# Moving the tiles that TensorE reads to multiples of 64 bytes, and spacing out the steps of the first block sums

## The chip, the cores and the metric

The kernel runs on one core of a Trainium2 chip. The metric is the device time of one execution in microseconds (us); the runs of one kernel are given by their median and their range. A profile of one execution shows each engine's instructions: PE is TensorE (PEld its weight loads), DVE is VectorE, ACT is ScalarE, POOL is GpSimd, SP issues the DMAs.

## The reference

Three stages follow each other, all in float32.

```python
# q, k, v: (8, 8, 576, 64); p: (8, 8, 32, 64)
p_packed = sm_attn(p, k, v)            # softmax attention of 32 packs per head
out = sm_attn(q, p_packed, p_packed)   # and back to 576 positions
x = out.transpose(0, 2, 1, 3).reshape(4608, 512)

xn = x / sqrt(mean(x * x) + 1e-6) * rms_g
g = xn @ w_gate                        # 512 -> 1536
x = (g * sigmoid(g) * (xn @ w_val)) @ w_out

h = x @ w_in                           # 512 -> 2048
return (h * sigmoid(1.702 * h)) @ w_out2
```

## The kernel before

**Precision.** A float32 value is kept as a rounded high part and a low part (tiles ending in h and l, or a tile with an index for the part), and a product is three matmuls: high by high, high by low, low by high.

**Stages.** The first MLP runs in four units of two batches each, `u` = 0 to 3. In each unit 12 column blocks of 128 follow: `prods` makes the gate and value weights of the unit on PE (ps_w, L668), `gateval` multiplies them with the attention weights (ps_g, L701; tanh on ACT at L708, two steps on DVE at L709 and L711 give the tile th, which is split into Hh on ACT and Hl on POOL), and `project`, called for two blocks at once, multiplies by w_out (ps_o, L732). The attention of the next unit runs between these steps, and so does the conversion of the weights: first those of the first MLP (`piece`), then those of the second (`weights` in `mlp2`), which go through a ring of three buffers with the tag raw (`RAWS`). The last unit has no attention of a next unit beside it; in its place stand the first block sums of the second MLP.

**The second MLP** works on 1024 tokens at a time (four times, then 512 tokens once) and on pairs of blocks of the hidden size (eight). The up product of a pair is a block matrix product in seven instead of eight block products (`up`, ps_up, L999): for this the tokens' inputs are seven tiles x_b11, x_b21, x_b22, x_t1, x_t2, x_t3 and x_t4, four of which are sums or differences of blocks. Each block product is six matmuls with 512 moving columns (256 for the last 512 tokens). The moving operand is the x_ tile, the stationary one a block of the weights (wi, or a staging tile for the first pair). Then `down` (ps_dn, L1062) multiplies the result by w_out2: 48 matmuls of 512 columns per pair (24 for the last 512 tokens), whose moving operand is the tile wo2 and whose stationary one is gh or gl. The down products of a pair are written between the up products of the next.

**The first 1024 tokens' sums** are made in `first_x` during the last unit of the first MLP. It is a generator of 11 steps: loads, splits into high and low part (`split_x`: a cast on ACT, a difference on DVE or POOL), and differences. The main loop calls one step at each step of the first MLP, from the start of the last unit on:

```python
if ahead is not None and u == NU - 1:
    next(ahead, None)
```

One difference goes into `spare()`, a buffer of the raw ring, and is split into x_t4 afterwards; the tile of t2 is free for its own split only once it has been read for that.

**What sets the order.** The kernel is written in one order, but a scheduler, which the framework runs while the program is built, decides where an instruction stands on its engine: one that is ready for its inputs and its buffers can be moved ahead of others that were written before it. Nothing is changed at run time; each engine works through its list.

**PSUM and SBUF.** The first MLP's products have five PSUM banks (pool mm). The pool `at` of attention, and after it the pool `pre` with the seven x_ tiles, lie at the right end of SBUF and are filled from that end; a tile's size therefore sets the address of all the tiles to its left.

Of the kernel before, what the change touches and what calls it, by code (L numbers as in the profile page):

```python
# [9 lines left out]
F32 = mybir.dt.float32  # L10
# [12 lines left out]
def fl(t):  # L23

    return t.bitcast(F32)
# [3 lines left out]
def tile_pack_attention__then__two_mlps(  # L29
# [14 lines left out]
    nc = tc.nc  # L44
    B, H, S, D = q.shape
# [8 lines left out]
    P = 128  # L54
# [16 lines left out]
    FULL = 4  # L71
# [15 lines left out]
    if NT % (2 * TH):  # L87
        spans.append((WHOLE * 2 * TH, NT % (2 * TH) // 2))
    SECOND = 4300.0
    SCALE = 1.0 / math.sqrt(D)  # L90

    dram = ctx.enter_context(tc.tile_pool(name="dram", bufs=1, space=DRAM))
# [46 lines left out]
    def attention(at, first, lp, psum, getL, getAT):  # L139
# [12 lines left out]
        def split(parts, src, engine):  # L152
            nc.scalar.copy(parts[0], src)
            if len(parts) > 1:
                engine.tensor_sub(parts[1], src, fl(parts[0]))
# [225 lines left out]
        def s2(n, e):  # L381
            b, g = chains[n]
            ps = scores(st[n]["ppT"], st[n]["qT"], e)
            if e == 0:
                st[n]["t"] = at.tile([P, S // 32, 32], F32, tag="e", name="t1", bufs=2)
            t = st[n]["t"]
            nc.vector.transpose(t[:, span(e).start // 32 : span(e).stop // 32, :], ps)
            if e == 0:
                return
            bc = [P, S // 32, 32]  # L390
            mx = at.tile([P, S // 32], F32, tag="mx", name="mx")
            nc.vector.tensor_reduce(mx, t, axis=AX.X, op=ALU.max)
            nc.gpsimd.tensor_sub(t, t, mx.unsqueeze(2).to_broadcast(bc))
            nc.scalar.activation(t, t, AF.Exp, scale=SCALE)
            sm = at.tile([P, S // 32], F32, tag="s2", name="s2")
            nc.vector.tensor_reduce(sm, t, axis=AX.X, op=ALU.add)
            nc.gpsimd.tensor_scalar_add(sm, sm, 1e-9)
            r2 = at.tile([P, S // 32], F32, tag="r2", name="r2")
            nc.vector.reciprocal(r2, sm)
            if n != NG:  # L400
                nc.gpsimd.tensor_mul(t, t, r2.unsqueeze(2).to_broadcast(bc))
            st[n]["r2"] = r2

        def weights(n):

            b, g = chains[n]
            A = getAT(b // 2)[b % 2][g]
            if n == NG:

                t = st[n]["t"]  # L410
                with behind(("ri", 0)):
                    nc.gpsimd.tensor_mul(t, t, st[n]["r2"].unsqueeze(2).to_broadcast([P, S // 32, 32]))
            nc.vector.transpose(A, st[n]["t"].rearrange("p t n -> p (t n)"))
            if full(n):
                st[n]["A"] = (A,)
                return
            st[n]["A"] = [at.tile([P, S], F32R, tag=f"A{x}", name=f"A{x}") for x in "hl"]
            split(st[n]["A"], A, nc.gpsimd)

        def x(n, c0):  # L420
# [394 lines left out]
    def mlp2(cv):  # L815
# [77 lines left out]
        def split_x(q, src, engine, n=TH):  # L893
            t = x_tile(q, n)
            nc.scalar.copy(t[:, 0], src)
            engine.tensor_sub(t[:, 1], src, fl(t[:, 0]))

        def first_x():

            t0, n = spans[0]  # L900
            a, b = (
                pools["pre"].tile([P, 2, 2, TH], F32, tag=q, name=f"x_{q}", bufs=1) for q in ("t4", "t2")
            )
            b11, b12, b22, b21 = a[:, 0], a[:, 1], b[:, 0], b[:, 1]
            for t, i0, k in ((b11, 0, 0), (b12, 0, 1), (b22, 2, 1), (b21, 2, 0)):
                load_part(t, i0, t0 + k * n, n)
            yield
            split_x("b11", b11, nc.gpsimd)
            yield
            nc.vector.tensor_sub(b11, b12, b11)  # L910
            nc.gpsimd.tensor_sub(b12, b22, b12)
            yield
            split_x("t1", b11, nc.vector)
            yield
            split_x("t3", b12, nc.gpsimd)
            yield
            split_x("b21", b21, nc.vector)
            yield
            split_x("b22", b22, nc.gpsimd)
            yield  # L920
            nc.vector.tensor_sub(b11, b22, b11)
            yield
            t4 = spare()
            nc.vector.tensor_sub(t4, b21, b11)
            yield
            split_x("t2", b11, nc.gpsimd)
            yield
            split_x("t4", t4, nc.vector)
            yield

        def first_w():
# [176 lines left out]
    pools = {}  # L1108
    with ExitStack():
# [9 lines left out]
        with ExitStack() as st1:  # L1119
# [4 lines left out]
            at = st2.enter_context(tc.tile_pool(name="at", bufs=1, side="right"))  # L1124
# [48 lines left out]
                todo = [calls for _, calls in todo]  # L1173
            starting[0] = False
            pools["main"] = st1.enter_context(tc.tile_pool(name="main", bufs=1, side="left"))
            u, ahead = 0, None
            sources = [mm]
            between = lambda: sources[-1]
            weights, first_x, first_w, second = mlp2(cv)
# [3 lines left out]
            for what in run():  # L1183
# [7 lines left out]
                elif what == "unit":  # L1191
# [4 lines left out]
                    elif u + 1 == NU:  # L1196
                        st2.close()
                        pools["pre"] = ctx.enter_context(tc.tile_pool(name="pre", bufs=1, side="right"))
                        ahead = first_x()
                    spent = 0.0  # L1200
                else:
                    if ahead is not None and u == NU - 1:
                        next(ahead, None)
                    spent += what
                    done += what
                    while todo and spent >= every:
# [5 lines left out]
                    if finished():  # L1212
                        ready += what
                        while ready >= SECOND:
                            ready -= SECOND
                            next(converting, None)
# [50 lines left out]
```

## Time and profile before

| | us |
|---|---|
| median of 3 runs | 1693.5 |
| range of the runs | 1692.46 to 1696.78 |
| profiled execution, time | 1693.33 |
| profiled execution, span of its instructions | 1691.4 |
| attention and first MLP, units 0 to 2 | 0 to about 731 |
| first MLP, last unit | about 731 to 934 |
| second MLP | 934 to 1691.4 |

Times within the profile are microseconds from the start of the span; 1.9 us of the execution lie outside it. A row that gives a line with an L names a line of the kernel; in tile names the buffer numbers are left out, so that x_t stands for x_t1 to x_t4 and x_b for x_b11, x_b21 and x_b22.

### The profile page before, as it was taken

The numbers are of one execution on the slowest core, as the hardware profiler recorded it, in microseconds if no ns is written. First come the engines' busy times: TensorE is split into PE (matmuls) and PEld (weight loads), VectorE is DVE, ScalarE is ACT, GpSimd is POOL, SyncE is SP. The second block draws the span as 40 slices with busy tenths as digits, with TensorE's granted clock in tenths as the row PEclk, the third lists the DMA queues.
The fourth block names the chain that finished last, engine by engine and source line by source line (L and its number), as shares of the span: only waits on it lengthen the run. The fifth ranks groups of instructions, "written<-read, shape, count | busy, mean of one in ns | idle before, by whom it ended". The sixth has DMA issues, their size and how long they took to land.

```text
span 1691.4 us, 25480 instructions
## 1 busy us (share of the span) xinstructions
PE 1649.5 (98%) x9312; PEld 1465.1 (87%) x9312; DVE 1148.6 (68%) x2154; ACT 730.7 (43%) x1586; POOL 719.3 (43%) x680
## 2 busy tenths in 40 slices
PE   7899999999999999989999999999999999999998
PEld 5689998999999999979999788888888888888897
DVE  5788988777878787877765355845584558455755
ACT  4667776666566665555554311321132113211221
POOL 2447777647664566574455211411141114111211
PEclk8999999999999999989999999999999999999999
DMA  9555666575655655466453833443344334333374
GB/s 267 158 174 175 205 185 227 196 231 173 184 206 172 228 170 179 167 212 216 171 194 110 314 137 137 144 162 137 137 153 153 137 137 143 138 137 137 135 267 152
DMA packets 163740, 298.41 MB, mean 176 GB/s; under 512 B 88992, under 2 KB 118688, under 8 KB 148384
## 3 DMA queue, kind: packets, MB, share of 16 engines
q1 hardware_dynamic: 163616, 296.79, 52.1%
q8 instruction: 74, 1.21, 0.3%
q14 instruction: 50, 0.41, 0.1%
HBM read 235.93 MB, written 60.82 MB: 175 GB/s over the span
## 4 chain that ended last, share of the span: by engine, by line
PE 85%; DVE 5%; DMA 3%; ACT 2%; issue 2%; POOL 1%; SPq 1%; DVEq 0%; POOLq 0%; ACTq 0%
PE ps_dn L1062 23%; PE ps_up L999 21%; PE ps_o L732 16%; PE ps_g L701 13%; PE ps_w L668 3%; PE ps_at L299 2%; PE ps_at L344 2%; PE ps_at L288 2%; PE ps_at L432 1%; DMA raw<-in_moe_w_out_dram 1%; SPq L174 1%; DMA vn<-in_v_dram 1%; DVE Wl L673 1%; DVE th L709 1%; DVE th L711 1%
## 5 line engine op out<-in xcount | busy, mean ns | idle before, releaser
L1044 POOL TENSOR_TENSOR gl<-gf,gh 128x512 fp32r<-128x512 f32 (+1 forms) x120 | 148.3, 1237 | 529.8 <-DVE gh L1043 527.9
L1062 PE MATMUL ps_dn<-wo,gh 128*128 128x512 f32 x1152 | 356.4, 393 | 1.1 <-DVE gh L1043 1.1
L732 PE MATMUL ps_o<-Hh,wo 128*128 128x384 f32 x1152 | 323.7, 342 | 11.6 <-DVE th L709 3.5
L1071 DVE TENSOR_TENSOR acc<-acc,ps_dn 128x512 f32<-128x512 f32 x252 | 172.4, 686 | 163.2 <-PE ps_dn L1062 161.9
L1062 PEld LDWEIGHTS ps_dn<-wo,gh 128*128 128x128 f32 x1152 | 214.6, 188 | 49.6 <-DVE gh L1043 1.3
L1041 ACT ACTIVATE gf<-gf 128x512 f32<-128x512 f32 (+1 forms) x120 | 70.8, 590 | 399.9 <-DVE gf L1023 245.6
L701 PE MATMUL ps_g<-Aqh,Wh 128*128 128x288 f32 x768 | 232.8, 304 | 3.3 <-ACT add L745 1.4
L732 PEld LDWEIGHTS ps_o<-Hh,wo 128*128 128x128 f32 x1152 | 212.3, 190 | 16.8 <-DVE th L709 4.1
L701 PE MATMUL ps_g<-Aql,Wh 128*128 128x288 f32 x768 | 226.0, 295 | 0.0
L701 PE MATMUL ps_g<-Aqh,Wl 128*128 128x288 f32 x768 | 225.4, 295 | 0.0
L999 PE MATMUL ps_up<-x_t,wi 128*128 128x512 f32 (+1 forms) x936 | 224.9, 371 | 0.0
L1062 PE MATMUL ps_dn<-wo,gl 128*128 128x512 f32 x576 | 222.0, 390 | 0.0
L732 PE MATMUL ps_o<-Hl,wo 128*128 128x384 f32 x576 | 196.3, 341 | 1.2 <-POOL Hl L718 1.2
L999 PEld LDWEIGHTS ps_up<-x_t,wi 128*128 128x128 f32 x936 | 165.5, 188 | 34.3
L718 POOL TENSOR_TENSOR Hl<-th,Hh 128x576 fp32r<-128x576 f32 x96 | 139.3, 1452 | 118.1 <-ACT Hh L717 115.4
L673 DVE TENSOR_TENSOR Wl<-ps_w,Wh 64x512 fp32r<-64x512 f32 x192 | 131.8, 687 | 68.8 <-ACT Wh L672 65.7
L999 PE MATMUL ps_up<-x_b,wi 128*128 128x512 f32 (+1 forms) x702 | 165.1, 372 | 0.4 <-ACT gf L1041 0.4
L747 POOL TENSOR_TENSOR acc<-acc,add 128x384 f32<-128x384 f32 x135 | 137.3, 1029 | 60.6 <-ACT add L745 59.1
L701 PEld LDWEIGHTS ps_g<-Aqh,Wh 128*128 128x128 f32 x768 | 144.0, 188 | 9.0 <-ACT add L745 1.7
L672 ACT CAST Wh<-ps_w 64x512 fp32r<-64x512 f32 x192 | 111.9, 583 | 85.9 <-PE ps_w L668 59.8
L999 PEld LDWEIGHTS ps_up<-x_b,wi 128*128 128x128 f32 x702 | 123.5, 188 | 26.4 <-issue 0.8
L701 PEld LDWEIGHTS ps_g<-Aql,Wh 128*128 128x128 f32 x768 | 144.3, 188 | 0.0
(185 smaller groups left out, 2995.7 us busy)
## 6 DMA issues: line engine op xcount, KB each, us to landing
wi<-wi SPq DMA_DIRECT2D x35, 1792.0 KB, 7.3
wg<-wg SPq DMA_DIRECT2D x48, 1024.0 KB, 5.7
wo<-wo SPq DMA_DIRECT2D x36, 1024.0 KB, 6.9
wo<-wo SPq DMA_DIRECT2D x48, 512.0 KB, 4.0
raw<-in_moe_w_out_dram SPq DMA_DIRECT2D x28, 512.0 KB, 4.6
wi<-stage SPq DMA_DIRECT2D x24, 512.0 KB, 5.2
x<-acc SPq DMA_DIRECT2D x32, 288.0 KB, 3.0
out_dram<-acc SPq DMA_DIRECT2D x36, 256.0 KB, 2.1
```

Of the source, the lines that this page charges most:

```text
L668: last = nc.tensor.matmul(ps[:, a], st[:, i], mv[:, i], start=n == 0, stop=n == 2)
L672: nc.scalar.copy(Wh[rows, :, g], src)
L673: nc.vector.tensor_sub(Wl[rows, :, g], src, fl(Wh[rows, :, g]))
L701: nc.tensor.matmul(ps, st[:, o, g, c * P : (c + 1) * P], mv[:, g, cols], start=n == 0, stop=n == 3 * NG - 1)
L718: nc.gpsimd.tensor_sub(Hl, th, fl(Hh))
L732: nc.tensor.matmul(ps, st[:, m * P : (m + 1) * P], mv[:, cols], start=n == 0, stop=n == 3 * len(ss) - 1)
L747: nc.gpsimd.tensor_add(a, a, t)
L999: nc.tensor.matmul(bank[b], wt[:, y, k], x[:, z, k], start=c == 0 and not go_on, stop=c == 5, skip_group_check=go_on)
L1041: nc.scalar.activation(gf, src, AF.Gelu_apprx_sigmoid)
L1044: engine.tensor_sub(gl, gf, fl(gh))
L1062: nc.tensor.matmul(ps, st[:, r * P : (r + 1) * P], w[:, i, y], start=c == 0, stop=c == 5)
L1071: nc.vector.tensor_add(acc[m], acc[m], ps)
```

## The change

The diff does two things. In three places it makes a pool 32 bytes a partition larger (the tile s2 grows from 72 to 128 bytes, where it took 96 with its padding; `even` is added to the pool `at` and `even2` to the pool `pre`), which moves the tiles to their left. And a step of `first_x` is called only after each 9000 ns of the loop's own count of matmul time (`CALM`), in place of at each step.

```diff
+    CALM = 9000.0
...
-            sm = at.tile([P, S // 32], F32, tag="s2", name="s2")
+            sm = at.tile([P, P // 4], F32, tag="s2", name="s2")[:, : S // 32]
...
             st[n]["A"] = [at.tile([P, S], F32R, tag=f"A{x}", name=f"A{x}") for x in "hl"]
+            if n == FULL:
+                nc.gpsimd.memset(at.tile([P, 8], F32, name="even"), 0.0)
             split(st[n]["A"], A, nc.gpsimd)
...
             split_x("t4", t4, nc.vector)
+            nc.gpsimd.memset(pools["pre"].tile([P, 8], F32, name="even2"), 0.0)
             yield
...
-            u, ahead = 0, None
+            u, ahead, calm = 0, None, 0.0
...
                     if ahead is not None and u == NU - 1:
-                        next(ahead, None)
+                        calm += what
+                        if calm >= CALM:
+                            calm -= CALM
+                            next(ahead, None)
```

In the built program the seven x_ tiles begin 32 bytes past a multiple of 64 before (x_t4 at 172000, the others 8192 bytes apart from 180192 on) and at a multiple of 64 now (171968, and from 180160 on). The tiles wo2, wi, gh and gl, and all that the first MLP's matmuls read, begin at multiples of 64 in both. In attention the tiles pbm, pTh, pTl, kTl, qTl, vh, vl, aTh, aTl, pp, ppl, ppTl, Ah, Al and the kept ones move from 32 past to a multiple of 64.

The order of the instructions changes less than the loop. This is DVE before, at the start of the last unit; x_t on the left of an arrow at L910 and L921 is a difference of blocks, x_b and x_t at L896 are the low parts of x_b21 and x_t1, Aql and th belong to the first MLP:

```order
L685 TENSOR_TENSOR Aql<-AT_7143,Aqh 128x576
L711 SCALAR_TENSOR_TENSOR th<-th,ps_g 128x288
L910 TENSOR_TENSOR x_t_10094<-x_t_10094 128x1024
L685 TENSOR_TENSOR Aql<-AT_7144,Aqh 128x576
L896 TENSOR_TENSOR x_b_10171<-x_t_10095,x_b_10171 128x1024
L742 TENSOR_TENSOR acc_7469<-acc_7469,ps_o 128x384
L673 TENSOR_TENSOR Wl<-ps_w,Wh 64x2x256
L896 TENSOR_TENSOR x_t_10147<-x_t_10094,x_t_10147 128x1024
L673 TENSOR_TENSOR Wl<-ps_w,Wh 64x2x256
L921 TENSOR_TENSOR x_t_10094<-x_t_10095,x_t_10094 128x1024
```

And this is DVE now at the same place, with the lines three further down:

```order
L688 TENSOR_TENSOR Aql<-AT_7145,Aqh 128x576
L714 SCALAR_TENSOR_TENSOR th<-th,ps_g 128x288
L913 TENSOR_TENSOR x_t_10226<-x_t_10226 128x1024
L688 TENSOR_TENSOR Aql<-AT_7146,Aqh 128x576
L899 TENSOR_TENSOR x_b_10823<-x_t_10227,x_b_10823 128x1024
L745 TENSOR_TENSOR acc_7471<-acc_7471,ps_o 128x384
L676 TENSOR_TENSOR Wl<-ps_w,Wh 64x2x256
L899 TENSOR_TENSOR x_t_10584<-x_t_10226,x_t_10584 128x1024
L676 TENSOR_TENSOR Wl<-ps_w,Wh 64x2x256
L924 TENSOR_TENSOR x_t_10226<-x_t_10227,x_t_10226 128x1024
```

Nothing has moved here: the four instructions of the sums have the same neighbours.

Before, the split of t4 (x_t from spare, at L896) stood on DVE at the end of a step's row of th products, some 30 rows further on, ahead of a weight conversion (between, L119 to L122):

```order
L709 SCALAR_TENSOR_TENSOR th<-th,ps_g 128x288
L711 SCALAR_TENSOR_TENSOR th<-th,ps_g 128x288
L709 SCALAR_TENSOR_TENSOR th<-th,ps_g 128x288
L711 SCALAR_TENSOR_TENSOR th<-th,ps_g 128x288
L896 TENSOR_TENSOR x_t_10233<-spare,x_t_10233 128x1024
L119 TENSOR_SCALAR between<-w 128x512
L120 TENSOR_SCALAR between<-between 128x512
L709 SCALAR_TENSOR_TENSOR th<-th,ps_g 128x288
```

Now the row of th products runs into the conversion without it:

```order
L712 SCALAR_TENSOR_TENSOR th<-th,ps_g 128x288
L714 SCALAR_TENSOR_TENSOR th<-th,ps_g 128x288
L712 SCALAR_TENSOR_TENSOR th<-th,ps_g 128x288
L714 SCALAR_TENSOR_TENSOR th<-th,ps_g 128x288
L120 TENSOR_SCALAR between<-w 128x512
L121 TENSOR_SCALAR between<-between 128x512
L122 SCALAR_TENSOR_TENSOR between<-raw_10173,between 128x512
L712 SCALAR_TENSOR_TENSOR th<-th,ps_g 128x288
```

The difference into spare and the split of t4 now stand on DVE about 100 rows further on, where a step's th products begin after the last low parts of the weights (Wl); acc is an accumulator of the first MLP, sums are sums of weight blocks of the second:

```order
L745 TENSOR_TENSOR acc_10401<-acc_10401,ps_o 128x384 x2
L927 TENSOR_TENSOR spare<-x_t_10227,x_t_10226 128x1024
L676 TENSOR_TENSOR Wl<-ps_w,Wh 64x2x256
L853 TENSOR_TENSOR sums<-sums,w 128x256
L745 TENSOR_TENSOR acc_10401<-acc_10401,ps_o 128x384
L676 TENSOR_TENSOR Wl<-ps_w,Wh 64x2x256
L854 TENSOR_TENSOR sums<-w,sums 128x256
L712 SCALAR_TENSOR_TENSOR th<-th,ps_g 128x288 x2
L676 TENSOR_TENSOR Wl<-ps_w,Wh 64x2x256
L714 SCALAR_TENSOR_TENSOR th<-th,ps_g 128x288 x2
L899 TENSOR_TENSOR x_t_11440<-spare,x_t_11440 128x1024
L712 SCALAR_TENSOR_TENSOR th<-th,ps_g 128x288 x2
```

Between its neighbours here the difference (L927) and the split (L899) are new; the casts that belong to the splits of t2 and t4 on ACT, and the difference of t2 on POOL, have moved to the same place.

## Rows read from the trace of the kernel before

**Rows 1.** The page: PE and the others over the span, granted clock in 40 slices.
```profile
PE 1649.5 (98%) x9312; PEld 1465.1 (87%) x9312; DVE 1148.6 (68%) x2154; ACT 730.7 (43%) x1586; POOL 719.3 (43%) x680
...
PEclk8999999999999999989999999999999999999999
```

**Rows 2.** The page: the chain that ended last, shares by line.
```profile
PE ps_dn L1062 23%; PE ps_up L999 21%; PE ps_o L732 16%; PE ps_g L701 13%; PE ps_w L668 3%; PE ps_at L299 2%; PE ps_at L344 2%; PE ps_at L288 2%; PE ps_at L432 1%; DMA raw<-in_moe_w_out_dram 1%; SPq L174 1%; DMA vn<-in_v_dram 1%; DVE Wl L673 1%; DVE th L709 1%; DVE th L711 1%
```

**Rows 3.** Stretches (from:to, length): busy time by engine, clock, DMA share.
```profile
core 0: us, PE busy (x) PEld busy (x) DVE busy (x) ACT busy (x) POOL busy (x), PEclk, DMA share, GB/s
505.00:545.00 40.00, 39.78 (x278) 38.41 (x277) 33.56 (x70) 25.11 (x60) 18.16 (x19) 1.00 0.50 171
730.00:765.00 35.00, 27.73 (x152) 25.54 (x150) 30.07 (x41) 19.57 (x33) 24.65 (x14) 0.85 0.52 177
765.00:790.00 25.00, 22.94 (x144) 22.51 (x145) 20.15 (x36) 13.38 (x25) 10.61 (x7) 0.93 0.51 179
...
934.00:1600.00 666.00, 665.56 (x2888) 539.87 (x2888) 376.52 (x576) 144.01 (x224) 160.71 (x109) 1.00 0.41 152
...
844.00:857.00 13.00, 13.00 (x92) 13.00 (x91) 11.57 (x21) 8.06 (x18) 7.33 (x8) 1.00 0.68 228
```

**Rows 4.** The chain in order of time, second MLP: start, length, what and count.
```profile
939.86 3.97 PE ps_up L999 x17
...
980.63 1.39 PE ps_dn L1062 x6
982.02 1.40 PE ps_up L999 x6
983.42 2.75 PE ps_dn L1062 x12
...
1004.27 2.75 PE ps_dn L1062 x12
```

**Rows 5.** PE's timeline in a long run of down products: start, length, instruction.
```profile
951.55 0.61 PE L1062 MATMUL ps_dn<-wo,gh 128*128 128x512 f32 x2
...
955.18 0.39 PE L1062 MATMUL ps_dn<-wo,gl 128*128 128x512 f32 x1
955.40 1.80 PE L999 MATMUL ps_up<-x_b,wi 128*128 128x512 f32 x7
```

**Rows 6.** The chain in order of time, first MLP.
```profile
786.36 3.12 PE ps_o L732 x18
789.48 0.71 PE ps_w L668 x6
...
907.89 12.72 PE ps_g L701 x96
920.61 12.49 PE ps_o L732 x72
```

**Rows 7.** The chain in order of time, last 512 tokens of the second MLP.
```profile
1615.17 4.20 PE ps_up L999 x36
...
1625.60 4.20 PE ps_up L999 x36
```

**Rows 8.** Tile x_t, 730 to 800 us: durations ns (min/median/max), first and last start.
```profile
L895 ACT CAST x_t<-x_t x3: 1042/1046/1047, 741.5 to 768.0; 128x1024 fp32r<-128x1024 f32 x3
...
L896 POOL TENSOR_TENSOR x_t<-x_t,x_t x2: 2393/2901/3409, 748.6 to 770.4; 128x1024 fp32r<-128x1024 f32 x2
...
L896 DVE TENSOR_TENSOR x_b<-x_t,x_b x1: 3380/3380/3380, 742.0 to 742.0; 128x1024 fp32r<-128x1024 f32 x1
...
L924 DVE TENSOR_TENSOR spare<-x_t,x_t x1: 1221/1221/1221, 766.7 to 766.7; 128x1024 f32<-128x1024 f32 x1
L895 ACT CAST x_t<-spare x1: 1048/1048/1048, 773.4 to 773.4; 128x1024 fp32r<-128x1024 f32 x1
L896 DVE TENSOR_TENSOR x_t<-spare,x_t x1: 2156/2156/2156, 774.5 to 774.5; 128x1024 fp32r<-128x1024 f32 x1
```

**Rows 9.** PE's waits, 730 to 765 us: us in total, times, longest.
```profile
PE ps_o L732 <- ACT add L745: 2.4, 1, 2.4
```

**Rows 10.** PE's waits, 765 to 790 us.
```profile
PE ps_o L732 <- DVE th L709: 2.0, 1, 2.0
```

## The prediction

> **What bounds the kernel now.** I read the shares of busy time first. PE is busy 98% of the span at a granted clock of nearly ten tenths throughout [rows 1], so the kernel can get faster in two ways only: PE's matmuls follow each other more closely, or the few stretches in which PE stands still go. The chain that ended last says the same: its longest lines, 23% and 21% of the span, are the down and the up products of the second MLP on PE, and the next three are PE's too [rows 2].
>
> The table of stretches shows where PE stands still [rows 3]. In the last unit's opening, 730 to 765 us, PE is busy 27.73 of 35 us at a mean clock of 0.85; from 765 to 790 it is busy 22.94 of 25 us at 0.93. The same passage one unit earlier, 505 to 545 us, is all but full (39.78 of 40, clock 1.00), and so is a stretch later in the last unit, 844 to 857. So what costs there is what only the last unit has, the block sums. In the second MLP, 934 to 1600 us, PE is busy 665.56 of 666 us: there only the pace of the matmuls counts.
>
> **The pace of the matmuls.** The chain in order of time gives it, since a piece divided by its count is the distance from start to start. In a steady iteration of the second MLP [rows 4] six up products take 1.40 us, 233 ns each; a run of 17 at the stage's start takes 3.97 us, also 233 ns, so this is no edge effect. Six down products between them take 1.39 us, 231.7 ns. But a long run of down products is faster: in PE's timeline [rows 5] from the first start at 951.55 us to the next up product at 955.40 there are 17 products in ten rows (the first and the last stand there), 226.5 ns each. That is 6.7 ns less than the up products', for the same 512 moving columns, 128 stationary columns, type and clock, with nothing waited for. What differs: the down products' moving tile (wo2) begins at a multiple of 64 bytes, the up products' (x_...) 32 bytes past one; both stationary tiles begin at a multiple. The down products behind up products share the slower pace for about six matmuls.
>
> Is it only the switch from one product to another? In the first MLP, where all tiles are aligned, ps_o products take 3.12 us for 18 between ps_w products, and 12.49 us for 72 in one run [rows 6]: 173.3 and 173.5 ns. There switching costs nothing.
>
> **The change, part by part. (1) Alignment in the second MLP.** The seven x_... tiles move down by 32 bytes; the counts of products stay. Of 40 iterations 32 have 42 up products of 512 columns, 1344 in all, and 48 down; the last eight have 42 up of 256 columns, 336, and 24 down. One iteration (42 up, 48 down) now takes 20.85 us (983.42 to 1004.27 [rows 4]). If all 90 ran at the pace of the long down run it would take 90 x 0.2265 = 20.39 us, 0.465 us less, and over 32 such iterations 14.9 us. In the eight last iterations, of 256-column up products, one takes 10.43 us (1615.17 to 1625.60 [rows 7]): 36 up in 4.20 us, 116.7 ns, so 42 x 0.1167 + 24 x 0.2265 = 10.34 us, 0.09 us less, together 0.7 us. The bounds are 0 (the gap has another cause) and 15.6 us. I take 15.6: the gap is there from the run at 939.86 us on [rows 4], when the weights still come out of a staging tile and no down product has run yet, and alignment is the one difference that lasts.
>
> A page of the Trainium skill speaks against this: Advanced Engine Details and Errata, section SBUF Cachelines, gives lines of 16 bytes. 32 bytes past a multiple of 64 is still the start of such a line, so by that rule no line more is touched and this term would be zero. The rows show a gap between 226.5 and 233 ns that this rule does not explain, but no run here has yet tied it to the address.
>
> **(2) Alignment in attention.** In the program some 680 matmuls of the attention stages also read a moved tile, all with 320 columns or fewer. The nearest rows are the 256-column products: 116.7 ns with a misaligned x_... tile [rows 7], 118 ns for the aligned ps_w (six in 0.71 us [rows 6]). So I price these at 0. Bounds: 680 x 6.7 ns = 4.6 us gained, or 1.6 ns lost on each and on the 336 short up products, 1.6 us.
>
> **(3) The spread.** The kernel text now asks for a step of the sums every 9 us of matmul work, but the order of the instructions hardly follows. In DVE's order the difference x_t4, the splits into x_b21 and x_t1 and the second difference stand between the same neighbours as before; on ACT and POOL the first five splits do too. These make the stall of 730 to 765 us: one split holds DVE for 3.38 us [rows 8], and of the 7.3 us that PE stands still there [rows 3] most are four waits for DVE and ACT, the longest 2.4 us [rows 9]. I price this at 0 change.
>
> Only what hangs on the ring of three raw buffers moves: the difference into `spare` (1.22 us [rows 8]) and the splits t2 and t4 (on ACT 1.05 us each, on POOL 2.39 at the least, on DVE 2.16 [rows 8]). On DVE they go from 766.7 and 774.5 us to where 850 and 856 us are now.
>
> What goes: at 774.5 us the t4 split holds DVE for 2.16 us just as the last th of a step is due; PE then waits 2.0 us for th [rows 10] and the clock falls. From [rows 3], 25 - 22.94 = 2.1 us idle, and a mean clock of 0.93 over 25 us is 3.5 us at the lower of the two levels, 1.75 us of lost work: 3.8 us.
>
> What comes: from 844 to 857 us DVE is busy 11.57 of 13 us and PE 13.00 [rows 3], and now 1.22 + 2.16 = 3.4 us of DVE work and two 1.05 us casts on ACT are added. Behind them on DVE wait the th products of a gate step and the last Wl, and PE waits for those through the five banks of pool mm. A ps_g group takes 12.72/16 = 0.8 us (96 matmuls [rows 6]), so five banks cover some 3 us of lateness, and the two DVE pieces stand apart with five rows of other work between. Bounds: 0, and 3.4 us plus 1.75 us of lower clock, 5.1 us. I take 1.0 us, near the lower end, because the pieces land at the opening of a step, not at its close. Net gain 2.8 us. Two 32-byte memsets on POOL add nothing: the second waits for a matmul that POOL's next instruction waits behind anyway.
>
> **Sum.** The profiled execution took 1693.3 us, at the median of the runs (1693.5). 1693.3 - 14.9 - 0.7 - 2.8 = 1674.9, so 1675 us.
>
> **Rivals.**
> *The address does not matter.* Then the 6.7 ns belong to the up products for a reason that stays, and only the 2.8 us remain: 1690.5 us. For it: the 256-column products read the same misaligned tiles at no loss. The Trainium skill's rule on lines gives the same. Against it: the pieces in [rows 4, 5]. Chance 0.30.
> *Only the up products heal.* If the down products behind them stay slow because the two alternate, the gain is 1344 x 6.7 ns = 9.0 us: 1693.3 - 9.0 - 2.8 = 1681.5. The runs in the first MLP [rows 6] speak against a price of alternating. Chance 0.10.
> *The moved splits make a new stall.* With the address worth nothing, the upper bound for the new place gives 1693.3 - 3.8 + 5.1 = 1694.6, slower than before. This decides once th is more than some 3 us late at 850 to 860 us, so that PE stands still long enough for the clock to fall. DVE's 1.4 free us of 13 speak for it, the order at the opening of a step against. Chance 0.05.
> *The steps do spread on the chip.* Then the loss of [rows 3] in 730 to 765 us goes as well: 7.3 us idle and 0.15 x 35 us = 5.2 us of clock, and 1675 becomes 1662.5. The order of instructions speaks against it. Chance 0.03.
>
> **How the numbers follow.** The forecast has 0.52, and its own range is 1671 (attention gains too) to 1680. The whole range reaches through the second rival into the first one's lower half: 1671 to 1692. What is left out, under 2 in 10, is the steps spreading, the new stall, and the end of the first rival where the moved splits gain little. No change means within 0.3%, 5.1 us, about what a measurement of this kernel can tell. Forecast, second and last rival lie beyond it: 0.65 faster. The other two lie within, but for 0.02 of worse stalls: 0.33 and 0.02.
>
> **What would show it.** In the chain after, six up products should take 1.36 us, not 1.40, and an iteration 20.4 us, not 20.85. If these pieces stay, the first rival holds. If up falls to 1.36 and down stays at 1.39, it is the second. The windows 730 to 765 us should look as before (the steps still bunched), and 765 to 790 us should reach clock 1.00 without the split on DVE. The moved split should stand near 852 us (what precedes is 3 to 4 us earlier), with PE's waits for th there under 1 us in all. The up products should begin about 3 us before 933.8 us. It would all be wrong if PE's pace were set by something both products share after the change, or if the late splits met a step's close.

## The result and the profile after

The changed kernel takes 1680.8 us (median of 4 runs, 1678.12 to 1680.88) against 1694.6 us of the kernel before (median of 4, 1692.46 to 1696.78): a ratio of 0.9915, 95% interval 0.9897 to 0.9932. The forecast was 1675 us with a range of 1671 to 1692, so the time lies in the range and the sign is right, but it is 5.8 us above the forecast and just outside the forecast's own range of 1671 to 1680. By the time alone the second rival, 1681.5 us, would look right; the trace below rules it out. The profiled execution took 1680.88 us, with a span of 1679.1 us; that is 12.45 us less than the 1693.33 us that the sum of the prediction began with.

Three points in the trace show in which part the time changed: the start of the first up product, the start of the first up product of 256 columns (the last 512 tokens), and the end of the span.

| part | before | after | change | forecast |
|---|---|---|---|---|
| up to the second MLP | 933.79 | 934.85 | +1.06 | -2.8 |
| to the first 256-column up product | 656.77 | 642.81 | -13.96 | -14.9 |
| from there to the end | 100.89 | 101.42 | +0.53 | -0.7 |

So the largest term came as forecast, and both small ones have the wrong sign.

The page after: PE's busy time fell by 12 us and its share stayed (compare [rows 1]).

```profile
PE 1637.6 (98%) x9312; PEld 1467.1 (87%) x9312; DVE 1149.7 (68%) x2154; ACT 729.8 (43%) x1586; POOL 716.0 (43%) x682
```

The chain in order of time in a steady iteration (start, length, what and count), to be read against [rows 4]:

```profile
980.78 1.36 PE ps_dn L1066 x6
982.14 1.36 PE ps_up L1003 x6
983.50 2.72 PE ps_dn L1066 x12
...
1003.90 2.72 PE ps_dn L1066 x12
```

Six up products take 1.36 us, where they took 1.40, and the six down products beside them 1.36, where they took 1.39: both kinds now follow each other at 226.7 ns. An iteration takes 1003.90 - 983.50 = 20.40 us; the forecast was 20.39.

The same view in the last 512 tokens, against [rows 7]:

```profile
1602.26 4.31 PE ps_up L1003 x36
1606.58 2.29 PE ps_dn L1066 x10
...
1612.79 4.31 PE ps_up L1003 x36
```

Here 36 up products take 4.31 us, where they took 4.20: 119.7 ns each in place of 116.7. Down products behind them take 229 ns each, not 226.5. An iteration takes 10.53 us, where it took 10.43.

The stretches of [rows 3] after (busy time by engine, clock, DMA share), and one more, 790 to 930 us:

```profile
core 0: us, PE busy (x) PEld busy (x) DVE busy (x) ACT busy (x) POOL busy (x), PEclk, DMA share, GB/s
505.00:545.00 40.00, 39.78 (x277) 38.40 (x277) 33.39 (x71) 25.18 (x60) 17.86 (x19) 1.00 0.51 176
730.00:765.00 35.00, 27.04 (x147) 24.80 (x145) 30.23 (x41) 18.80 (x33) 23.93 (x13) 0.85 0.53 183
765.00:790.00 25.00, 24.73 (x155) 24.29 (x156) 18.51 (x36) 13.18 (x27) 8.22 (x7) 0.94 0.45 170
844.00:857.00 13.00, 11.45 (x79) 11.21 (x78) 12.40 (x21) 7.92 (x14) 7.55 (x6) 1.00 0.70 246
790.00:930.00 140.00, 136.90 (x927) 135.56 (x927) 93.42 (x174) 71.81 (x143) 73.39 (x64) 1.00 0.47 163
```

The same last stretch in the kernel before:

```profile
790.00:930.00 140.00, 139.43 (x946) 138.44 (x945) 91.44 (x174) 72.00 (x145) 72.27 (x64) 1.00 0.48 167
```

The opening, 730 to 765 us, stayed as it was. From 765 to 790 us PE stands still for 0.27 us in place of 2.06. But from 790 to 930 us it now stands still for 3.10 us in place of 0.57, half of it (1.55) between 844 and 857 us, where the moved pieces now stand.

The tile x_t after, 725 to 870 us (durations min/median/max in ns, first and last start), against [rows 8]:

```profile
L913 DVE TENSOR_TENSOR x_t<-x_t x1: 3034/3034/3034, 737.7 to 737.7; 128x1024 f32<-128x1024 f32 x1
L899 DVE TENSOR_TENSOR x_b<-x_t,x_b x1: 3386/3386/3386, 741.3 to 741.3; 128x1024 fp32r<-128x1024 f32 x1
...
L899 DVE TENSOR_TENSOR x_t<-spare,x_t x1: 1219/1219/1219, 857.0 to 857.0; 128x1024 fp32r<-128x1024 f32 x1
```

The two long pieces at the opening are still there. The t4 split moved to 857.0 us, as the order said, and is shorter there (1.22 us, where it took 2.16).

PE's waits (us in total, times, longest) from 755 to 785, 825 to 845 and 845 to 865 us; the row of [rows 10] is gone:

```profile
PE ps_g L704 <- DVE th L712: 1.8, 1, 1.8
...
PE ps_o L735 <- ACT add L748: 1.3, 1, 1.3
...
PE ps_g L704 <- DVE th L712: 1.6, 1, 1.6
```

What is late in the first and the last of them, from the timelines of ACT, DVE and POOL (start, length, instruction, in brackets the idle time before it and what ended it):

```profile
760.55 0.66 ACT L119 ACTIVATE w<-raw 128x512 f32<-128x512 f32 x1 [3.08 <-DMA raw<-in_moe_w_out_dram]
761.24 0.58 ACT L675 CAST Wh<-ps_w 64x512 fp32r<-64x512 f32 x1
...
852.98 1.79 DVE L854 TENSOR_TENSOR sums<-w,sums 128x256 f32<-128x256 f32 x1
...
852.10 2.39 POOL L899 TENSOR_TENSOR x_t<-x_t,x_t 128x1024 fp32r<-128x1024 f32 x1 [2.60 <-ACT x_t L898]
```

At 760.5 us ACT has waited 3.1 us for a block of raw weights, with the cast Wh and the tanh of a gate step behind it in its list; DVE's th is then late and PE waits. At 853 us it is not the split of t4 that holds th up: it starts at 857.0. The piece ahead of th is a sum of weight blocks that takes 1.79 us, where the same sum (L851 before) took 0.42, while POOL makes the other moved split, that of t2, beside it.

### The profile page after: what moved, and what is told of

Read it like the earlier page. It is cut to its first block, busy times and chain, and to the rows that moved or that the text cites. A ratio compares the mean times of both kernels' runs of the same rounds, so it can differ in the third digit from the quotient of the medians.

```text
span 1679.1 us, 25485 instructions
## 1 busy us (share of the span) xinstructions
PE 1637.6 (98%) x9312; PEld 1467.1 (87%) x9312; DVE 1149.7 (68%) x2154; ACT 729.8 (43%) x1586; POOL 716.0 (43%) x682
## 4 chain that ended last, share of the span: by engine, by line
PE 85%; DVE 6%; DMA 3%; ACT 2%; issue 1%; POOL 1%; SPq 1%; DVEq 0%; POOLq 0%; ACTq 0%
PE ps_dn L1066 23%; PE ps_up L1003 20%; PE ps_o L735 15%; PE ps_g L704 14%; PE ps_w L671 3%; PE ps_at L300 2%; PE ps_at L345 2%; PE ps_at L289 2%; DMA vn<-in_v_dram 2%; PE ps_at L435 2%; SPq L175 1%; DMA raw<-in_moe_w_out_dram 1%; DVE Wl L676 1%; DVE between L120 0%; DVE th L712 0%
## 5 line engine op out<-in xcount | busy, mean ns | idle before, releaser
L1066 PE MATMUL ps_dn<-wo,gh 128*128 128x512 f32 x1152 | 352.1, 390 | 1.1 <-DVE gh L1047 1.1
L1003 PE MATMUL ps_up<-x_t,wi 128*128 128x512 f32 (+1 forms) x936 | 220.8, 367 | 0.0
L1003 PE MATMUL ps_up<-x_b,wi 128*128 128x512 f32 (+1 forms) x702 | 161.6, 367 | 0.5 <-ACT gf L1045 0.5
L704 PEld LDWEIGHTS ps_g<-Aqh,Wh 128*128 128x128 f32 x768 | 144.6, 188 | 12.2 <-DVE th L712 4.2
L704 PEld LDWEIGHTS ps_g<-Aqh,Wl 128*128 128x128 f32 x768 | 144.4, 188 | 0.0
```

Of the source, the lines that this page charges most:

```text
L704: nc.tensor.matmul(ps, st[:, o, g, c * P : (c + 1) * P], mv[:, g, cols], start=n == 0, stop=n == 3 * NG - 1)
L1003: nc.tensor.matmul(bank[b], wt[:, y, k], x[:, z, k], start=c == 0 and not go_on, stop=c == 5, skip_group_check=go_on)
L1066: nc.tensor.matmul(ps, st[:, r * P : (r + 1) * P], w[:, i, y], start=c == 0, stop=c == 5)
```

## The experiments

The two theories. **The address:** the pace of the 512-column products follows from where the moving tile starts, so the alignment of the seven x_ tiles brings nearly the whole gain, and calling the steps at larger distances brings nothing, since the steps did not spread. **The rival:** the address does not matter, and what was gained is due to other instructions standing beside each other.

All kernels but e5 in one table. e1 to e4 ran on one chip, e5 and e6 on one, e7 and e8 on one. Ratios are to runs of the kernel before on the same chip (its medians there were 1692.7 to 1693.6 us), with 95% intervals; "starts" is the first up product in the traced execution, "unit 2 on" the time from the first ps_w product of unit 2 to that point, "512" and "256" are the two parts of the second MLP as above, and "half clock" is the time from 730 to 860 us for which the trace has the granted clock at the lower level; all in us.

| kernel | median | ratio | starts | unit 2 on | 512 | 256 | half clock |
|---|---|---|---|---|---|---|---|
| before | 1694.6 | | 933.8 | 411.7 | 656.8 | 100.9 | 13.6 |
| changed | 1680.8 | 0.9915 (0.9897 to 0.9932) | 934.9 | 413.3 | 642.8 | 101.4 | 13.6 |
| e1, alignment alone | 1679.8 | 0.9919 (0.9906 to 0.9932) | 933.6 | 410.8 | 642.8 | 101.4 | 10.2 |
| e2, spread alone | 1693.4 | 1.0002 (0.9992 to 1.0011) | 931.7 | 413.1 | 656.3 | 100.9 | 10.2 |
| e3, x_ tiles alone | 1680.2 | 0.9927 (0.9914 to 0.9940) | 936.2 | 415.0 | 642.6 | 101.4 | 17.1 |
| e4, steps pinned | 1671.1 | 0.9871 (0.9856 to 0.9886) | 925.7 | 406.0 | 642.7 | 101.4 | 3.4 |
| e6, wo2 moved off | 1691.7 | 0.9997 (0.9988 to 1.0007) | 933.0 | 411.5 | 655.0 | 102.2 | 10.2 |
| e7, pinned, no spacing | 1674.6 | 0.9890 (0.9870 to 0.9909) | 928.0 | 406.7 | 642.8 | 101.4 | 3.4 |
| e8, pinned, short tiles off | 1672.0 | 0.9872 (0.9850 to 0.9894) | 927.5 | 405.8 | 642.9 | 100.9 | 3.4 |

The column "starts" has noise of its own: the traced executions reach the first ps_w product of unit 1 anywhere between 301.4 and 305.7 us, long before the steps of the sums. So what the last unit gains or loses is better read from "unit 2 on".

**e1, alignment alone.** The changed kernel with a step at each step of the loop:

```diff
-                        calm += what
-                        if calm >= CALM:
-                            calm -= CALM
-                            next(ahead, None)
+                        next(ahead, None)
```

> The tiles are moved, the steps of the sums are called as before. If the address sets the pace (theory), the second MLP takes 744 us as in the changed kernel, the opening of the last unit is that of before, and the time is about 13.4 us under before, near 1680, or some 1 us under the changed kernel. If the gain came from the spacing of the steps (rival), the time stays at before, 1694.

1679.8 us: the whole gain of the change, without the spread. The chain in order of time shows the new pace, 1002.66 - 982.26 = 20.40 us for an iteration:

```profile
982.26 2.72 PE ps_dn L1066 x12
...
1002.66 2.72 PE ps_dn L1066 x12
```

**e2, spread alone.** The kernel before with `CALM` and the four lines that use it, and no tile moved.

> The steps are spaced out, no tile is moved. Theory: the second MLP takes 757 us as before, the moved split makes its own stall near 853 us, and the time is 0 to 2 us over before. Rival (the spacing brought the gain): about 1681.

1693.4 us against 1693.6 of the kernel before. An iteration stays at 1001.67 - 980.83 = 20.84 us:

```profile
980.83 2.75 PE ps_dn L1063 x12
...
1001.67 2.75 PE ps_dn L1063 x12
```

In its one traced execution the second MLP began 2.1 us earlier than before, but that execution had reached unit 1 3.5 us earlier already, and the interval of the ratio allows the spread a gain of 1.4 us at most (0.0008 of 1693). The stall that was expected near 853 us is there: PE stands still for 1.5 us from 850.5 us on.

**e3, the seven x_ tiles alone.** The kernel before with one line more, so that nothing of attention moves and no step is spread:

```diff
             split_x("t4", t4, nc.vector)
+            nc.gpsimd.memset(pools["pre"].tile([P, 8], F32, name="even2"), 0.0)
```

> Only the seven x_ tiles are moved (the pad in the pool pre alone), the tiles of attention stay 32 bytes past a multiple of 64, the steps are called as before. Theory: within 1 us of the run in which all tiles are moved. Rival (the attention's matmuls gain as well, up to 4.6 us): up to 4.6 us above that run, and the start of the last unit later by as much.

1680.2 us, and 642.6 us in the 512-column part: 32 bytes in the start of seven tiles bring all of it. An iteration takes 1005.06 - 984.66 = 20.40 us:

```profile
984.66 2.72 PE ps_dn L1063 x12
...
1005.06 2.72 PE ps_dn L1063 x12
```

The alignment in attention, which e1 has and this kernel has not, shows no gain in the times (1679.8 against 1680.2, the intervals overlap). The traces settle it more closely. From the first ps_w product of unit 1 to that of unit 2, a stretch in which the attention of the next unit runs and the clock is full, it takes 217.16 us in the three kernels with attention's tiles 32 bytes past (before, e2, e3) and 217.18 to 217.23 in the six others.

**e4, the steps pinned.** The changed kernel with every cast and difference of `first_x` held where the program writes it:

```diff
+        def held(f, *args):
+            tc.keep_in_program_order(f(*args))
...
-            split_x("b11", b11, nc.gpsimd)
+            split_held("b11", b11, nc.gpsimd)
...
-            nc.vector.tensor_sub(b11, b12, b11)
+            held(nc.vector.tensor_sub, b11, b12, b11)
```

> The changed kernel, with every instruction of the sums held behind what was written before it on its engine, so that the steps stand spread over the last unit in the engines' lists too. If the bunching costs what the stretch of 730 to 765 us shows, its 7.3 us of standing still and some 5 us of lower clock go, and the time is some 8 to 12 us under the changed kernel, near 1670. Rival: each spread step makes its own stall of 1 to 2 us, as the one moved split did, and nothing or only 2 to 3 us is gained, 1678 or more.

1671.1 us, below both kernels: 8.7 us less than e1 on the same chip, and 9.7 less than the changed kernel's own runs. The steps now do spread (the six pieces on DVE start between 782.9 and 866.6 us), and the opening is nearly full. Stretches, as above:

```profile
core 0: us, PE busy (x) PEld busy (x) DVE busy (x) ACT busy (x) POOL busy (x), PEclk, DMA share, GB/s
730.00:765.00 35.00, 33.29 (x217) 31.42 (x216) 27.99 (x52) 19.21 (x38) 15.63 (x13) 1.00 0.70 260
765.00:790.00 25.00, 24.39 (x167) 24.39 (x168) 20.10 (x38) 14.11 (x29) 14.21 (x11) 1.00 0.54 191
```

PE stands still for 1.7 us where it stood still for 8.0, at full clock. Not all of that is kept: from 790 to 930 us it is idle for 4.9 us. From unit 2 on the traced execution takes 406.0 us, where the six kernels without pinning take 410.8 to 415.0. The split of x_b21, 3.39 us on DVE in the changed kernel, is another length here, in the view of the tile:

```profile
L902 DVE TENSOR_TENSOR x_b<-x_t,x_b x1: 1226/1226/1226, 812.1 to 812.1; 128x1024 fp32r<-128x1024 f32 x1
```

**e5, the pace by itself.** A kernel that computes nothing of the reference, with one run on record: runs of 24 products of float32 parts, the moving tile starting 0, 4, 16, 32 or 48 bytes past a multiple of 64, for several widths, with two stationary tiles at multiples of 64; then the aligned moving tile with a stationary tile 32 bytes past; then sixes of two kinds in turn.

```python
STARTS = {"zero": 0, "four": 1, "sixteen": 4, "half": 8, "late": 12}   # words past
m = nc.tensor.matmul(ps[:, :n], still[s], moving[name][:, :n], start=i % 6 == 0, stop=i % 6 == 5)
```

> Nothing of the kernel is computed: only matmuls of one high part by another, back to back, 24 for each of five starts of the moving tile (0, 4, 16, 32 and 48 bytes past a multiple of 64) and seven widths (512, 496, 480, 448, 384, 320, 256 columns), then a stationary tile 32 bytes past, then sixes of two kinds in turn. Theory: 512 columns take 226.7 ns at 0 and 233 at 32; 256 columns take 120 at 0 and 117 at 32. If a part more of 64 bytes has to be read where the tile begins past a multiple, 4, 16 and 48 cost the same as 32, and 496 columns at 32, which touch no more parts than 512 at 0, still cost more than 496 at 0. If only the reach past 32 such parts costs, 496 and fewer columns pay nothing. Rival, by lines of 16 bytes (the Trainium skill, Advanced Engine Details and Errata, SBUF Cachelines): 16, 32 and 48 take what 0 takes, and 4 alone costs more. The stationary tile's start: 0 in the theory.

PE's timeline (start, length, instruction and count); a run begins where the name of the moving tile changes:

```profile
12.12 0.61 PE L53 MATMUL ps<-mov_zero,still_sa 128*128 128x512 f32 x2
...
26.40 0.63 PE L53 MATMUL ps<-mov_four,still_sa 128*128 128x512 f32 x2
...
32.08 0.63 PE L53 MATMUL ps<-mov_sixteen,still_sa 128*128 128x512 f32 x2
...
37.63 0.62 PE L53 MATMUL ps<-mov_half,still_sa 128*128 128x512 f32 x2
...
43.22 0.62 PE L53 MATMUL ps<-mov_late,still_sa 128*128 128x512 f32 x2
...
48.81 0.61 PE L53 MATMUL ps<-mov_zero,still_sa 128*128 128x496 f32 x2
...
165.10 0.40 PE L53 MATMUL ps<-mov_zero,still_sa 128*128 128x256 f32 x2
...
167.98 0.41 PE L53 MATMUL ps<-mov_four,still_sa 128*128 128x256 f32 x2
...
173.72 0.40 PE L53 MATMUL ps<-mov_half,still_sa 128*128 128x256 f32 x2
...
176.52 0.40 PE L53 MATMUL ps<-mov_late,still_sa 128*128 128x256 f32 x2
...
179.36 8.59 PE L53 MATMUL ps<-mov_zero,still_sc 128*128 128x512 f32 x48
187.79 0.63 PE L53 MATMUL ps<-mov_half,still_sa 128*128 128x512 f32 x2
...
189.19 0.63 PE L53 MATMUL ps<-mov_zero,still_sa 128*128 128x512 f32 x2
...
190.57 0.63 PE L53 MATMUL ps<-mov_half,still_sa 128*128 128x512 f32 x2
```

From 12.12 to 26.40 us there are 63 aligned products, 226.7 ns each; the 24 from 26.40 to 32.08 take 236.7 ns each. Worked out in this way, in ns from start to start, at one granted clock (1.00), to about half a nanosecond:

| columns | 0 bytes | 4 | 16 | 32 | 48 |
|---|---|---|---|---|---|
| 512 | 226.7 | 236.7 | 231.3 | 232.9 | 232.9 |
| 496 | 223.7 | 229.6 | 223.3 | 224.6 | 224.2 |
| 480 | 217.1 | 220.0 | 216.7 | 220.0 | 213.3 |
| 448 | 206.3 | 206.7 | 202.1 | 206.3 | 202.9 |
| 384 | 174.6 | 173.3 | 175.0 | 173.8 | 174.6 |
| 320 | 146.7 | 152.1 | 145.8 | 146.7 | 146.3 |
| 256 | 120.0 | 122.5 | 116.7 | 116.7 | 118.3 |

With the stationary tile 32 bytes past and the moving one aligned, 24 products of 512 columns take 233.3 ns each (the first 24 of the 48 from 179.36 us on, up to 184.96 us), where the theory expected no price; 24 of 256 columns behind them take 117.9, less than the 120.0 with both aligned. In turns, a six of 512 aligned columns takes 230.7 ns a product behind a six that is 32 bytes past, and 231.3 behind an aligned six of 256 columns. So at 512 columns every start past 64 bytes costs 5 to 10 ns; at 496, 384 and 320 next to nothing does except 4 bytes at 496 and 320; at 480 and 448 it goes either way by up to 4 ns; at 256 an aligned start is the dearer one than 16 or 32 bytes past.

The paces expected at 0 and 32 bytes for 512 and 256 columns came out. Of the explanations that were put on record none holds at every width. That each start past a multiple costs a part more of 64 bytes fails at 496 columns, where 16, 32 and 48 bytes cost less than 1 ns. That only the reach past 32 such parts costs fails with 4 bytes at 496 and 320. Lines of 16 bytes fail at 512. No kernel here has both tiles of a 512-column product 32 bytes past, so whether the multiple of 64 counts or the equal start of the two operands is not shown.

**e6, wo2 moved off.** The changed kernel with the down products' moving tile 32 bytes past a multiple of 64, all else aligned:

```diff
-                    t = wp.tile([P, 2, 2, DM], F32R, tag="wo", name="wo2", bufs=3)
+                    t = wp.tile([P, 4 * DM + 16], F32R, tag="wo", name="wo2", bufs=3)
+                    t = t[:, 8 : 8 + 4 * DM].rearrange("p (i y d) -> p i y d", i=2, y=2)
```

> The changed kernel with the moving tile of the down products, wo2, 32 bytes past a multiple of 64, the x_ tiles at a multiple. Theory: the down products now take 233 ns and the up products between them are drawn along; an iteration takes 20.85 us or a little more in place of 20.39, and the time is 14 to 20 us over the changed kernel, 1695 to 1700. Rival (something else than the address makes the up products slow): the down products stay at 226.7 ns and the time at 1680.

1691.7 us: the gain is gone again, though the up products' tiles are aligned. The time is below the 1695 to 1700 us that were expected: the 512-column part takes 12.2 us more than in the changed kernel, where 14 to 20 were expected, because the up products beside the misaligned ones lose less: 229.7 ns in the mean of the part, against 227.3 in the changed kernel and 233.9 before. Iterations differ, from 20.70 to 20.91 us; this one in the chain takes 1005.60 - 984.69 = 20.91 us:

```profile
984.69 1.38 PE ps_up L1004 x6
...
997.20 1.41 PE ps_dn L1067 x6
...
1005.60 1.38 PE ps_up L1004 x6
```

The down products of this six now take 235 ns (232.7 in the mean of the part), and the aligned up products beside them 230: the slower pace passes to the neighbours in this direction too.

**e7, pinned without the spacing.** The pinned kernel with the edit of e1.

> The kernel with the instructions of the sums pinned to where the program writes them, but with a step of the sums at every step of the loop again, as before the change. Theory A, spacing and pinning are both needed: DVE's order has the six pieces of the sums within 34 rows (within some 100 with the spacing), so part of the stall near 740 to 765 us stays; the second MLP begins at 928 to 933 us (925.7 with the spacing, 934.9 in the changed kernel), 1673 to 1678 us in all. Rival B, pinning alone does it: begins at 925 to 927 us, 1670 to 1672 us. Rival C, pinning without spacing is worth nothing: 933 to 935 us, 1679 to 1681 us.

1674.6 us (1673.28 to 1676.61), in the range of theory A. Its ratio of 0.9890 stands between those of the changed kernel (0.9915) and e4 (0.9871), but its interval overlaps both. On the same chip e8, which has both pinning and spacing, took 1671.47 to 1673.05 us, and 0.5 us of that difference are e8's short tiles. In the traces e7 takes 406.7 us from unit 2 on, e4 406.0 and e8 405.8, against 410.8 to 415.0 without pinning. So pinning alone brings more than half of what both bring together; how much the spacing adds, less than 1 us by the traces and 2 to 3 by the medians, is not settled. The stretches show what is left of the stall, now from 765 to 790 us:

```profile
730.00:765.00 35.00, 31.92 (x210) 30.14 (x209) 30.86 (x52) 20.38 (x38) 18.86 (x13) 1.00 0.71 259
765.00:790.00 25.00, 21.44 (x121) 19.68 (x120) 22.20 (x32) 15.13 (x26) 17.56 (x10) 0.93 0.27 89
```

**e8, pinned, with the short moving tiles off.** The pinned kernel, where the x_ tiles of the last 512 tokens are read from 32 bytes past:

```diff
-            xb[q] = pools["pre"].tile([P, 2, 2, TH], F32R, tag=q, name=f"x_{q}", bufs=1)[:, :, :, :n]
+            xb[q] = pools["pre"].tile([P, 2, 2, TH], F32R, tag=q, name=f"x_{q}", bufs=1)
+            o = 8 if n < TH else 0
+            xb[q] = xb[q][:, :, :, o : o + n]
```

> The pinned kernel, with the moving tiles of the 256-column up products alone (the last 512 tokens) read from 32 bytes past a multiple of 64 again; all 512-column products stay aligned. Theory A, the start of the moving tile makes the short products slower: 36 up products take 4.20 us again (4.31 aligned), 116.7 ns each, and the last part of the second MLP, from its first up product to the end, takes 100.4 to 100.9 us (101.43 aligned). Rival B, what makes them slower is not their start: 4.31 us and 101.4 us stay. The time is 1670 to 1671 us under both, too near to tell them apart; the trace tells.

Theory A: the old 4.20 us are back, and an iteration takes 1605.41 - 1594.97 = 10.44 us. The last part is 0.5 us shorter than in e4. Down products stay at 229 ns.

```profile
1594.97 4.20 PE ps_up L1013 x36
1599.18 2.29 PE ps_dn L1076 x10
...
1605.41 4.20 PE ps_up L1013 x36
```

The time, 1672.0 us, is 1 us above the 1670 to 1671 that were expected and cannot be told from e4's (on another chip): in the traced execution the second MLP began 1.7 us later, and unit 1 had begun 1.9 us later already.

## Why the prediction was right and where it was wrong

**Alignment in the second MLP, 512 columns: right, mechanism and size.** The step was that all 90 products of an iteration would go at the pace of the long down run. They do: 20.40 us, forecast 20.39. Over 32 iterations that is 14.4 us; the part up to the first 256-column product holds 13.96 of them, which is 31 iterations' worth: the last pair's down products run behind that point. e3 shows that the start of the x_ tiles alone does it, e6 that the start of the other moving tile undoes it, and e5 that it happens without the rest of the kernel. The first rival (the address does not matter, 0.30) is refuted by these three; the second (only the up products heal) by the six down products at 1.36 us.

For the first rival the prediction had the rule of the Trainium skill on lines of 16 bytes (Advanced Engine Details and Errata, section SBUF Cachelines). At 512 columns the runs disagree with what was drawn from it: a start 16 bytes past costs 231.3 ns against 226.7, and 32 bytes cost 232.9. At 496 columns they agree: 16 bytes past cost nothing (223.3 against 223.7), and 4 bytes do (229.6); so they do at 320. The mechanism within the chip stays open.

**The last 512 tokens: wrong in sign, by a small term.** The step that failed is "42 x 0.1167 + 24 x 0.2265 = 10.34". It kept the up products at the 116.7 ns that they had with the misaligned tile, and let the down products heal. Neither happened. Aligned short products take 119.7 ns (e8 turns this back and forth with the start alone), and down products behind sixes of 256 columns take 229 to 231 ns whatever the start (e8, and the sixes in turn of e5). The prediction had seen the sign in its bounds, from ps_w at 118 ns, but priced it at 0. Measured: 10.53 us in place of 10.34. The count was too high as well. Only six iterations of the eight run at that step; the first 24.6 us of the part, where short up products stand in sixes between down products, take the same before and after (1590.56 to 1615.17 and 1577.66 to 1602.26). Six times 0.09 is the 0.5 us that the part shows.

**Attention: right at 0.** The times of e1 and e3 allow that, and the traced stretch from unit 1 to unit 2 shows it: 217.16 us with the old starts and 217.18 or a little more with the new ones.

**The opening of the last unit: right.** The steps did not spread, and the stretch from 730 to 765 us stayed as it was. e4 shows what a real spread is worth: some 9 us (the last rival, 1675 to 1662.5, had 12.5), of which e7 has more than half by the held order alone. What the last rival left out is that the steps cost something where they now stand: PE stands still for 4.9 us from 790 to 930 us.

**The two moved splits: wrong, 2.8 us of gain forecast, none measured.** The step "what goes: 3.8 us" took the stall at 774.5 us as lost time that the split alone caused. That stall did go from its place. The kernels compare three to three here. Without the spread (before, e1, e3) PE stands still for 1.5 to 2.0 us at 776 to 778 us and not at all between 844 and 857 us; with it (the changed kernel, e2, e6) it stands still for 0.3 us at the first place and for 1.5 to 1.6 us at the second. One stall was exchanged for another of nearly its size. From unit 2 on the three without the spread take 410.8 to 415.0 us and the three with it 411.5 to 413.3.

The 1.75 us of lower clock in the same step were not a fixed part of the price: the lower clock stands behind that stall in the kernel before (778.4 to 781.8 us), but behind the same stall in e1 and e3 it does not. In the changed kernel there is half clock from 764.5 to 767.9 us, behind a stall of 1.8 us at 761 us: PE waits there for what ACT makes behind raw weights that land at 760.5 us (760.3 before). This stall is not the change's. e3, without the spread, has it too (1.2 us), and e6, with it, has 0.6 us. The half clock from 730 to 860 us is 13.6 us in the kernel before and in the changed one, 10.2 in e1, e2 and e6, and 17.1 in e3; only pinning takes it down (3.4 us in e4, e7 and e8). That the weights' landing is what stands behind the stall at 761 us is read from the traces; no run here moved that transfer.

The step "what comes: 1.0 us" named the right place and the wrong carrier. The wait at 853 us is 1.6 us, inside the bounds of 0 and 5.1 but over the 1 us that was named as a sign, as the clock of 0.94 from 765 to 790 us is under the 1.00 that was named. DVE was held by a sum of weight blocks that took four times as long beside the split on POOL. The prediction counted the split on DVE and left out what the split on POOL does to DVE's other work.

Together: 18.4 us of gain were forecast, and the profiled execution has 12.45. The two parts of the second MLP gave 13.4 of the 15.6 forecast, so 2.2 are missing there; what lies ahead of it gave 1.1 of loss in place of 2.8 of gain, 3.9 us. Of these 3.9 the 2.8 are the gain that was not there; the 1.1 are within what single executions differ by (e4 and e8, the same up to the second MLP, enter it 1.7 us apart). That the spread alone gains nothing to be told is shown by e2.

## What to carry to other kernels

Before taking PE as full, divide its chain pieces by their counts for each pair of operands: two groups of the same shape that differ by 3% can point at where a tile starts, and a pad of 32 bytes is a cheap way to find out. At 512 columns start both operands at multiples of 64 bytes, and measure shorter widths, since at 256 columns the better start was another one. Do not take a time that lands near a forecast for its mechanism: the second rival's time was nearer than the forecast's, and only the chain told them apart. A step that a program calls later is not later on the engine unless the order of the instructions says so: read the order, and pin it where the spacing is the purpose. When a stall is taken away from a stretch that has several, price the gain by the sum of the stalls in a run without it, not by the one stall, and ask what the moved work does where it lands.

## What the runs showed of the hardware

- The stationary tile's start costs as much as the moving one's: 233.3 ns against 226.7 at 512 columns, although its load has only 128 columns (e5). At 256 columns it has the sign of the moving one's too (117.9 against 120.0).
- The pace of a six depends on the six before it: an aligned six of 512 columns behind a misaligned one takes 230.7 ns a product (e5), and in e6 the aligned up products 230. It is not the start alone that does this, since behind an aligned six of 256 columns it is 231.3 (e5); behind aligned sixes of 512, in the changed kernel, it is 226.7.
- The price depends on the width without a simple pattern: 6 ns at 512 columns, about 1 at 496, 3 at 480, none at 448, 384 and 320, -3 at 256, each for 32 bytes past. From 256 to 512 aligned columns the time grows by 106.7 ns, 0.417 ns a column, one period of the upper level (2.4 GHz). What is over, 120.0 - 106.7 = 13.3 ns at both widths, is 13 to 15 ns at 320 and 384 too, but 17 to 20 at 448 to 496.
- The same DVE difference of 128x1024 elements took 3.39 us in the opening, where POOL makes its own differences at the same time, and 1.23 us in e4 at a place where POOL stands still; a sum of 128x256 took 0.42 us before and 1.79 beside POOL's split. The lengths fit one of the two waiting for the other. The piece that started second takes its own length and what the first had still to run, less some 0.15 us. In the changed kernel DVE's difference at 741.34 us began with 2.31 us of POOL's to run (1.22 + 2.31 = 3.53, measured 3.39), and the sum at 852.98 us with 1.51 (0.42 + 1.51 = 1.93, measured 1.79). The other way round, POOL's split at 747.89 us began with 1.18 us of a DVE difference to run (2.39 + 1.18 = 3.57, measured 3.41), and that DVE difference kept its 1.23. A DVE difference that reads PSUM, Wl at 745.12 us, kept its 0.68 us beside POOL. This is read from one trace; no run here moved two such pieces apart.
